# Six float32 units in the first token tile, a shorter pooled attention branch and a split PSUM pool in an attention and two-layer kernel

## The chip, the cores and the metric

The kernel runs on one core of one Trainium2 chip. The metric is the device time of one execution in microseconds (us); the time before is the median of three runs.

## What is computed

```python
q, k, v: (4, 8, 576, 64) float32          # batch, heads, positions, width
# attn(q, k, v): softmax(q @ k.T / 8) @ v
out_d  = attn(q_d, k_d, v_d)              # q_d, k_d, v_d: means of 4 positions (144 rows)
local  = attn(q, k, v) where |i - j| < 4, all other scores -1e9
x = np.repeat(out_d, 4, axis=2) + local   # then laid out as 2304 tokens x 512
h = x @ moe_w_in                          # 512 x 2048, weights arrive as float64
x = softplus(h) @ moe_w_out               # 2048 x 512
h = x @ moe2_w_in
return (h * cos(h)) @ moe2_w_out          # 2304 x 512 float32
```

## The kernel before

**Tiles and stages.** The 2304 tokens lie in five tiles, four of 512 and one of 256. Each of the two layers works a tile in 16 units of 128 hidden columns. One unit is a product into the hidden columns (`unit_in`, "in-unit"), an activation, and a product out of them (`l2` for layer 1, `l4` for layer 2, "out-group": one unit has two halves). A float32 factor is kept as a float16 high part and a float16 low part, and a product of two such factors is made of three float16 products (high by high, high by low, low by high), so that an in-unit is 12 products of 128x128 by 128x512 (L1028) and each half of an out-unit 6 (L1119 in layer 1, L1154 in layer 2).

**Weights.** They arrive as float64 words in `stg` buffers, two units (one block) per DMA. ScalarE rebases a block (L553), VectorE joins the words to float32 (L425, L561), ScalarE sums up a bound (L569), from which a power-of-two scale is fitted (the bounds of four blocks go through a product with an identity, L464, to spread them over the partitions), then ScalarE makes the high half (L440) and VectorE the low one (L436). The first out-group waits for the low halves of W_out's first block.

**Attention.** A pair is two heads of one batch entry; there are 16, `p00` to `p33`, and the first four give tile 0. The stages of one pair, as the code names them: sum1, sum2 (VectorE pools q and k by four, L428, `qt` and `qd`), sum3, sum4 (the same for v), A (local scores, L703 and L707, in windows of 58 rows by 64 keys), A2 to A6 (largest, subtract, exp, sum, normalise), B (pooled scores: three products of 96x144, L761, out of a `qd` whose halves are padded with zeros), B1 to B4, C and D (transposes of the two attention matrices, L809 and L826), E (products with v: pooled L849, windows L860), `up` and E1 (the sum, L874). Tile 0 goes to `raw0`; its scale comes from a bound on v (`vmx`, L693), and is known before the attention is.

**Order.** `Plan` lists operations with estimated costs, works out due times backwards, adds the offsets of the table MOVES, and lists the operations engine by engine; the resulting order of each engine is fixed. Wherever the planner sees TensorE idle it adds a filler, a product of zeros (L1330). POS1 to POS3 say after which unit a later pair is entered in the list. PSUM has three double banks (`any`) and two single ones (`h`). All DMAs are issued by SyncE (SP).

Of the kernel before, what the change touches and what calls it, by code (L numbers as in the profile page):

```python
# [28 lines left out]
RB = 2 * SD // 3  # L29
# [11 lines left out]
POS1 = (6, 10, 15, 20)  # L41
POS2 = (33, 37, 41, 45)
POS3 = (50, 55, 60, 65)
# [14 lines left out]
QKP, VP = (), ()  # L58
YIN = 8
DR4 = 4  # L60
A_W, A_C, A_X, A_G = True, True, True, False
CAP = ("pe", "dve", "act")
OUT0 = 10
IN0 = ((0, 4), (4, 4))

MOVES = {
# [51 lines left out]
class Op:  # L118
    def __init__(self, n, cost, fn, claim, name):
        self.n, self.cost, self.fn, self.claim, self.name = n, cost, fn, claim, name  # L120
        self.succ, self.wait, self.values = set(), 0, set()
        self.key = ""


class Plan:
# [109 lines left out]
    def order(self):  # L235
# [22 lines left out]
        while left:  # L258
            held, started = set(), False
            for op in ready:  # L260
# [18 lines left out]
                if e == "sp":  # L279
                    end = max(dma_free, now + 1.1) + op.cost[e]  # L280
                    dma_free = end
                    free[e] = max(now + 0.45, end - 1.3)
                else:
                    end = now + op.cost[e]
                    free[e] = end
                op.eng, op.start, op.end = e, now, end
# [20 lines left out]
            while done and done[0][0] <= now:  # L307
# [7 lines left out]
                heapq.heappush(done, (end + LAT[op.eng], -1 - n, op))  # L315
                for s in op.succ:
# [41 lines left out]
def build(tc, qk, vw, vd, mask, w1i, w1o, w2i, w2o, out):  # L358
# [3 lines left out]
    with ExitStack() as ctx:  # L362
# [4 lines left out]
        small = ctx.enter_context(tc.tile_pool(name="small", bufs=8))  # L367
# [15 lines left out]
        vmx = const.tile([128, NC_], BF16, name="vmx")  # L383
# [12 lines left out]
        BANK = ring(ps, "any", 3, [128, 2, 512])  # L396
        HB = ring(ps, "h", 2, [128, 512])
# [6 lines left out]
        QT, QD = ring(ap, "qt", 1, [128, 2, SD, 2]), ring(ap, "qd", 2, [128, 3 * SD])  # L404
        VS, SM = ring(ap, "vs", 3, [72, 4, 64]), ring(ap, "sm", NSM, [128, NG, 2, 64])
        ED, AT = ring(ap, "ed", 2, [RB, 3, SD]), ring(ap, "aT", 1, [128, NG, 128])
        AD, UP = ring(ap, "aTd", 1, [72, 2, 2 * SD]), ring(ap, "up", 1, [128, SD])
# [8 lines left out]
        for t in QD.tiles:  # L416
            nc.gpsimd.memset(t[64:128, 0:SD], 0.0)
            nc.gpsimd.memset(t[0:64, SD : 2 * SD], 0.0)
# [35 lines left out]
        def allmax(am, n, red, reads, writes, name):  # L454
# [4 lines left out]

            h = HB.new()  # L460

# [7 lines left out]
            def top():  # L469
                red.append(small.tile([128, 4], F32, tag="red", name="red")[:, 0:n])  # L470
# [29 lines left out]
        class Weight:  # L500
            def __init__(self, name, dram):
                self.name, self.dram, self.first = name, dram, name[1] == "1"
                self.bd, self.s = carr(f"bd_{name}", NB, BF16), carr(f"s_{name}", NF)
# [8 lines left out]

            def hi(self, f, a, n):
                a += 2048 * (f // 2) + 512 * (f % 2)
                return self.t[:, a : a + n]

            def lo(self, f, a, n):
                return self.hi(f, 1024 + a, n)

            def his(self, b):  # L520
                return self.hi(2 * b, 0, 1024).rearrange("p (m e) -> p m e", m=2)

            def los(self, b):
                return self.lo(2 * b, 0, 1024).rearrange("p (m e) -> p m e", m=2)

            def floats(self, b):
                return self.t[:, 2048 * b + 1024 : 2048 * b + 3072].bitcast(F32).rearrange("p (m e) -> p m e", m=2)
# [7 lines left out]
            def decode(self, b, after=()):  # L535
# [30 lines left out]
                def bound():  # L566
# [829 lines left out]
```

## Time and profile before

| | |
|---|---|
| median of 3 runs | 898.52 us (895.9 to 900.05) |
| profiled execution, own time | 899.84 us |
| its span, mean granted TensorE clock | 898.1 us, 0.994 |
| TensorE busy | 870.8 us (97%) |
| weight loads | 453.8 us (51%) |
| VectorE busy | 651.1 us (73%) |
| ScalarE busy | 489.6 us (55%) |
| GpSimd busy | 1.6 us |

The profile is of one execution. Busy time is summed per engine over the whole span, so an engine that sets the pace of one stage can show a low share. TensorE's figure includes the fillers. The clock is the share of full speed that the chip granted to TensorE.

### The profile page before, as it was taken

The numbers are of one execution on the slowest core, as the hardware profiler recorded it, in microseconds if no ns is written. First come the engines' busy times: TensorE is split into PE (matmuls) and PEld (weight loads), VectorE is DVE, ScalarE is ACT, GpSimd is POOL, SyncE is SP. The second block draws the span as 40 slices with busy tenths as digits, with TensorE's granted clock in tenths as the row PEclk, the third lists the DMA queues.
The fourth block names the chain that finished last, engine by engine and source line by source line (L and its number), as shares of the span: only waits on it lengthen the run. The fifth ranks groups of instructions, "written<-read, shape, count | busy, mean of one in ns | idle before, by whom it ended". The sixth has DMA issues, their size and how long they took to land.

```text
span 898.1 us, 14241 instructions
## 1 busy us (share of the span) xinstructions
PE 870.8 (97%) x5699; PEld 453.8 (51%) x5699; DVE 651.1 (73%) x1342; ACT 489.6 (55%) x871; POOL 1.6 (0%) x11
## 2 busy tenths in 40 slices
PE   8888889999999999999999999999999999999997
PEld 4554445445555555444447764444444444445663
DVE  6989999956576856789994764857555675657662
ACT  3579999375453577689966642423234332334331
POOL 0000000000000000000000000000000000000000
PEclk9989999999999999999999999999999999999999
DMA  8764650301222000554400000001000100100001
GB/s 291 242 225 139 239 226 15 94 1 29 58 68 109 1 1 1 188 188 141 141 1 1 2 1 1 0 1 47 1 1 1 47 1 1 48 1 1 1 1 70
DMA packets 13361, 58.87 MB, mean 66 GB/s; under 512 B 1520, under 2 KB 1648, under 8 KB 9200
## 3 DMA queue, kind: packets, MB, share of 16 engines
q1 hardware_dynamic: 13296, 57.97, 18.8%
q8 instruction: 44, 0.72, 0.3%
q14 instruction: 21, 0.17, 0.1%
HBM read 53.25 MB, written 4.72 MB: 65 GB/s over the span
## 4 chain that ended last, share of the span: by engine, by line
PE 77%; ACT 9%; DMA 6%; DVE 6%; issue 1%; SPq 0%; ACTq 0%; DVEq 0%
PE h L1028 35%; PE any L1154 21%; PE any L1119 17%; DMA stg<-w1i 2%; ACT stg L569 2%; DMA stg<-w1o 2%; PE any L860 1%; DMA stg<-w2i 1%; ACT ta L1036 1%; ACT tb L1040 1%; ACT ta L1044 1%; ACT ta L1048 1%; DMA mask_sb<-mask 1%; PE any L761 1%; DVE w1i_t L561 1%
## 5 line engine op out<-in xcount | busy, mean ns | idle before, releaser
L1028 PE MATMUL h<-xt,w1i_t 128*128 128x512 f16 (+1 forms) x960 | 196.7, 358 | 5.5 <-ACT tb L1040 4.5
L1028 PE MATMUL h<-xt,w2i_t 128*128 128x512 f16 (+1 forms) x960 | 198.0, 358 | 0.0
L1154 PE MATMUL any<-w2o_t,g 128*128 128x512 f16 x864 | 197.2, 379 | 0.0
L1119 PE MATMUL any<-g,w1o_t 128*128 128x512 f16 (+1 forms) x864 | 175.4, 355 | 0.0
L1028 PEld LDWEIGHTS <-w1i_t 128*128 128x128 f16 x960 | 93.2, 98 | 97.1 <-issue 6.4
L1028 PEld LDWEIGHTS <-w2i_t 128*128 128x128 f16 x960 | 93.9, 98 | 94.9
L1061 ACT ACTIVATE ta<-h,quarter,i 128x512 f32<-128x512 f32 (+1 forms) x80 | 58.7, 734 | 146.3 <-PE h L1028 142.5
L1119 PEld LDWEIGHTS <-w1o_t 128*128 128x128 f16 x960 | 92.6, 98 | 85.5
L1154 PEld LDWEIGHTS <-g 128*128 128x128 f16 x864 | 84.4, 98 | 98.0
L428 DVE TENSOR_TENSOR g<-td,g 128x512 f16<-128x512 f32 (+1 forms) x152 | 96.2, 633 | 10.8 <-ACT g L446 4.7
L1066 DVE TENSOR_SCALAR tb<-ta 128x512 f32<-128x512 f32 (+1 forms) x80 | 32.0, 400 | 87.6 <-ACT ta L1061 87.4
L1072 ACT ACTIVATE tc<-ta 128x512 f32<-128x512 f32 (+1 forms) x80 | 46.9, 587 | 74.9 <-DVE ta L428 74.6
L1076 DVE SCALAR_TENSOR_TENSOR td<-h,r,tc 128x512 f32<-128x512 f32 (+1 forms) x80 | 55.8, 697 | 32.0 <-ACT tc L1072 29.4
L1036 ACT ACTIVATE ta<-h,i 128x512 f32<-128x512 f32 (+1 forms) x80 | 51.5, 644 | 34.9 <-PE h L1028 31.3
L436 DVE SCALAR_TENSOR_TENSOR td<-ta,sg,tb 128x512 f32<-128x512 f32 (+1 forms) x64 | 43.6, 682 | 23.5 <-ACT ta L1048 22.3
L1048 ACT ACTIVATE ta<-ta,one 128x512 f32<-128x512 f32 (+1 forms) x80 | 54.4, 684 | 1.4
L428 DVE TENSOR_TENSOR ta<-ta,tb 128x512 f32<-128x512 f32 (+1 forms) x80 | 51.1, 638 | 2.4
L1040 ACT ACTIVATE tb<-h,r 128x512 f32<-128x512 f32 (+1 forms) x80 | 51.4, 643 | 0.0
L448 DVE CAST g<-td 128x512 f16<-128x512 f32 (+1 forms) x109 | 42.5, 390 | 8.8 <-PE any L1154 2.6
L1044 ACT ACTIVATE ta<-ta 128x512 f32<-128x512 f32 (+1 forms) x80 | 47.1, 591 | 0.0
L446 ACT ACTIVATE g<-td 128x512 f16<-128x512 f32 (+1 forms) x43 | 26.2, 610 | 17.1 <-DVE td L1076 5.4
L1330 PE MATMUL h<-zero 128*128 128x512 f16 x106 | 30.8, 430 | 3.3 <-POOL zero L1321 2.4
(150 smaller groups left out, 820.7 us busy)
## 6 DMA issues: line engine op xcount, KB each, us to landing
qk<-qk SPq DMA_DIRECT2D x16, 589.0 KB, 5.4
stg<-w1i SPq DMA_DIRECT2D x8, 1024.0 KB, 4.8
stg<-w1o SPq DMA_DIRECT2D x8, 1024.0 KB, 6.6
stg<-w2i SPq DMA_DIRECT2D x8, 1024.0 KB, 6.4
stg<-w2o SPq DMA_DIRECT2D x8, 1024.0 KB, 4.9
vw<-vw SPq DMA_DIRECT2D x16, 320.0 KB, 3.3
vd<-vd SPq DMA_DIRECT2D x16, 288.0 KB
out<-osb SPq DMA_DIRECT2D x18, 256.0 KB, 2.0
```

Source lines behind the costliest of these rows:

```text
L428: eng[e].tensor_tensor(out=out, in0=in0, in1=in1, op=op)
L436: nc.vector.scalar_tensor_tensor(out=out, in0=raw, scalar=s, in1=other, op0=ALU.mult, op1=op)
L1028: nc.tensor.matmul(h.t[:, 0:n], l, r, start=(i == 0), stop=(i == 11))
L1036: act(n, 1, True), lambda: nc.scalar.activation(out=a(), in_=h.t[:, 0:n], func=AF.Abs, scale=col(o.i1, f)),
L1040: act(n, 1, True), lambda: nc.scalar.activation(out=b(), in_=h.t[:, 0:n], func=AF.Relu, scale=col(o.r1, f)),
L1044: act(n), lambda: nc.scalar.activation(out=a(), in_=a(), func=AF.Exp, scale=-1.0),
L1048: act(n, 1), lambda: nc.scalar.activation(out=a(), in_=a(), func=AF.Ln, bias=one),
L1061: act(n, 2, True), lambda: nc.scalar.activation(out=a(), in_=h.t[:, 0:n], func=AF.Identity, scale=col(o.i2, f), bias=quarter), [h, *sc], [ ...
L1072: act(n), lambda: nc.scalar.activation(out=r(), in_=a(), func=AF.Sin, scale=TWOPI),
L1076: dve(n, False, 1), lambda: nc.vector.scalar_tensor_tensor(out=td.t[:, 0:n], in0=h.t[:, 0:n], scalar=col(o.r1, f), in1=r(), op0=ALU.mult, ...
L1119: nc.tensor.matmul(a.t[:, i, 0:n], l, r, start=(first and j == 0), stop=(last and j == 2))
L1154: nc.tensor.matmul(a.t[:, i], l, r, start=(f == 0 and j == 0), stop=(f == NF - 1 and j == 2))
```

## The change

**Float32 units.** With `F0 = 6` the first six units of tile 0 use the joined float32 weights as they are: four float32 products per unit into the hidden columns (`first_in`, L1093), softplus without scales (ScalarE abs, exp, ln; VectorE G into a float32 `g`), and four float32 products per unit out (`first_out`, L1130). Their sum is copied to `xt[0]` ("ypart"), and the scaled sum of the other ten units is added to it. Units 0 and 1 issue their products one at a time (`PARTS = 2`). The weight blocks 0 to 2 of layer 1 are split into halves only after that, for tiles 1 to 4; the places of halves and float32 blocks in the weight tile change accordingly.

**Scale of tile 0.** It is now taken from the largest element of `raw0` (four reductions of 512 columns) in place of the four `vmx` reductions of 640.

**Pooled branch.** sum1 is one operation of 576 columns (was two of 288), sum2 one of 288 (was three of 144); the zeroed halves are gone. B is four products on 64 rows, two of 128x144 (L812) and two of 64x144 (L817). One add and one reciprocal on 13 columns serve both attentions (were four small operations). D's six transposes have 128 columns (were 96).

**Windows.** For batch entries 2 and 3 (`QUADS = 2`) E's window products alternate between the two halves of the rows; A3 becomes two operations and E1 more and smaller ones.

**PSUM.** A fourth double bank is there during the first pairs, in a pool of its own; after the fourth pair's E it is closed and opened again as the two `h` banks. `aT` and `aTd` get a second buffer each.

**Order.** POS1 to POS3 and MOVES are new (one line of many is shown), and the list of out-groups begins with the ten split units of tile 0.

```diff
+F0 = 6
+QUADS = 2
+PARTS = 2
-POS1 = (6, 10, 15, 20)
+POS1 = (1, 2, 4, 8)
...
-    "L1 0 0 ln#1": -56.5, "L1 0 10": -48.5, "L1 0 11": -31, "L1 0 11 exp#1": 132, "L1 0 11 gh#1": -28.5,
...
-                for a in range(2):
-                    two(e, qt.t[:, a], x[:, a, :, 0:2], x[:, a, :, 2:4], ALU.add)
+                two("dve", q, x[:, :, :, 0:2], x[:, :, :, 2:4], ALU.add)
...
-                for t in range(3):
+                for j in range(2):
+                    h = slice(64 * j, 64 * j + 64)
                     nc.tensor.matmul(
-                        bank()[0:RB, SD * t : SD * t + SD], qd.t[:, RB * t : RB * t + RB],
-                        qd.t[:, 2 * SD : 3 * SD], start=True, stop=True,
+                        pb.t[:, j, 0:SD], qd.t[h, 16 * j : 16 * j + 128], qd.t[h, SD : 2 * SD], start=True, stop=True
                     )
...
+                z = slice(64 * side(j, n // 2), 64 * side(j, n // 2) + 64)
...
+        def first_in(f):
...
+            def mm(cs):
+                for c in cs:
+                    nc.tensor.matmul(h.t, W1I.f32(f, 128 * c, 128), raw0[c], start=(c == 0), stop=(c == NC_ - 1))
...
+                    out=u.g(), in0=h.t, scalar=0.0, in1=ta.t, op0=ALU.max, op1=ALU.add
...
+        def first_out(f):
...
+                        nc.tensor.matmul(
+                            a.t[:, i], W1O.f32(f, 128 * (2 * d + i), 128), u.g(), start=first, stop=last
+                        )
...
-            first, last = f == 0, f == NF - 1
+            first, last = f == (0 if t else F0), f == NF - 1
```

The order of TensorE at the first product of tile 0 shows what stands ahead of the layer's first unit. In the names, `qd` and `ed` belong to pooled pairs, `sm` to a local one, `zero` to a filler, `raw` to tile 0; before:

```order
L761 MATMUL any_87<-qd_118 96x144 [waits DVE_49,Activation_49]
L761 MATMUL any_87<-qd_118 96x144 x2
L1330 LDWEIGHTS zero
L1330 MATMUL h_91<-zero 128x512
L1028 LDWEIGHTS w1i_t
L1028 MATMUL h_91<-xt_82,w1i_t 128x512
```

and with the change:

```order
L740 MATMUL any_83<-qk_108 64x64 [waits DMAHW2_49]
L740 MATMUL any_83<-qk_108 64x64 x19
L1093 MATMUL h_775<-raw_150,w1i_t 128x512 [waits DVE_49,PE_49]
L870 MATMUL any_84<-ident,ed_123 72x128 [waits DVE_49]
L870 MATMUL any_84<-ident,ed_123 72x128 x5
L1093 MATMUL h_775<-raw_151,w1i_t 128x512
L853 MATMUL any_85<-ident,sm_121 128x128 [waits Activation_49]
L853 MATMUL any_85<-ident,sm_121 128x128 x4
L1093 MATMUL h_775<-raw_152,w1i_t 128x512
L812 MATMUL any_84<-qd_116 128x144 [waits Activation_49]
L812 MATMUL any_84<-qd_116 128x144
L817 MATMUL any_84<-qd_116 64x144 x2
```

The first unit's products (three of four are shown) now stand one by one between the transposes of one pair and the scores and products of others, and no filler stands behind them; the last filler is six rows ahead of the first.

On VectorE, the operations up to the first low half of W_out (`w1o_t`), before (`td` is an activation, `sm` and `nm` attention, `s_w1o` and `k` scales):

```order
L436 SCALAR_TENSOR_TENSOR td_96<-ta_92,lc_160,tb_94 128x512 [waits DVE_49]
L425 TENSOR_SCALAR ik_167<-k_166 128x1 [waits DVE_49]
L428 TENSOR_TENSOR sm_124<-any_87,nm_219 128x640
L425 TENSOR_SCALAR s_w1o<-lc_160,k_166 128x16
L428 TENSOR_TENSOR xt_85<-td_96,xt_85 128x512 [waits Activation_49]
L724 TENSOR_REDUCE nm_220<-any_88 128x10
L436 SCALAR_TENSOR_TENSOR w1o_t<-w1o_t,s_w1o 128x1024 [waits Activation_49]
L436 SCALAR_TENSOR_TENSOR td_96<-ta_93,lc_160,tb_95 128x512 [waits DVE_49]
```

and with the change (`red` and `sx` belong to the scale of tile 1):

```order
L449 SCALAR_TENSOR_TENSOR td_94<-ta_90,lc_156,tb_92 128x512 [waits DVE_49,Activation_49]
L438 TENSOR_SCALAR s_w1o<-lc_156,k_162 128x10
L461 CAST xt_81<-td_94 128x512 [waits DVE_49]
L764 TENSOR_REDUCE nm_215<-any_83 128x10 [waits PE_49]
L441 TENSOR_TENSOR xt_81<-td_94,xt_81 128x512 [waits DVE_49]
L485 TENSOR_REDUCE red_236<-h_776 128x1 [waits PE_49]
L449 SCALAR_TENSOR_TENSOR w1o_t<-w1o_t,s_w1o 128x1024 [waits Activation_49]
L438 TENSOR_SCALAR sx_176<-red_236 128x1 [waits DVE_49]
```

The low half is the 277th VectorE instruction before, and the 234th with the change.

On TensorE, the place where the first split out-group begins, before:

```order
L703 MATMUL any_89<-mask_sb,ident_b 128x320
L707 MATMUL any_89<-qk_109 64x64 [waits DMAHW2_49]
L707 MATMUL any_89<-qk_109 64x64 x19
L1119 LDWEIGHTS w1o_t [waits Activation_49]
L1119 MATMUL any_87<-g_98,w1o_t 128x512 [waits DVE_49]
```

and with the change:

```order
L1159 LDWEIGHTS w1i_t
L1159 MATMUL h_776<-xt_78,w1i_t 128x512
L1130 MATMUL any_84<-g_100,w1o_t 128x512 x2
L1250 LDWEIGHTS w1o_t [waits Activation_49]
L1250 MATMUL any_85<-g_102,w1o_t 128x512 [waits DVE_49]
```

Where the scores of an attention pair stood ahead of the out-group, an in-unit of tile 0 and float32 out-products stand now; 22 of the 24 float32 out-products stand ahead of it.

## Rows read from the trace of the kernel before

**Rows 1.** The page: span of the profiled execution.
```profile
span 898.1 us, 14241 instructions
```

**Rows 2.** By stretch: sum; busy PE, PEld, DVE, ACT, POOL; TensorE clock, DMA share, GB/s.
```profile
0.00:147.20 147.20, 125.72 (x1326) 72.70 (x1326) 135.92 (x278) 113.37 (x231) 1.64 (x11) 0.97 0.62 210
64.00:147.20 83.20, 73.13 (x725) 40.72 (x722) 81.15 (x154) 80.26 (x158) 0.00 (x0) 1.00 0.49 175
147.90:893.50 745.60, 744.39 (x4343) 380.47 (x4333) 513.60 (x1064) 374.88 (x639) 0.00 (x0) 1.00 0.11 36
```

**Rows 3.** VectorE in order of time near 147 us: start, length, instructions [wait ahead].
```profile
145.96 1.28 DVE L436 SCALAR_TENSOR_TENSOR w1o_t<-w1o_t,s_w1o 128x1024 f16<-128x1024 f32 x1 [0.23 <-ACT w1o_t L440]
147.16 0.75 DVE L436 SCALAR_TENSOR_TENSOR td<-ta,lc,tb 128x512 f32<-128x512 f32 x1
```

**Rows 4.** TensorE in order of time near 148 us; x counts records.
```profile
147.22 0.81 PE L707 MATMUL any<-qk 64*64 64x64 f32 x40
147.96 20.89 PE L1119 MATMUL any<-g,w1o_t 128*128 128x512 f16 x96
168.69 4.05 PE L1119 MATMUL any<-xt,w1o_t 128*128 128x512 f16 x18
```

**Rows 5.** VectorE, groups by form up to 147.2 us: total, mean ns, idle before.
```profile
L436 DVE SCALAR_TENSOR_TENSOR td<-ta,lc,tb 128x512 f32<-128x512 f32 x14 | 10.4, 744 | 0.1
...
L724 DVE TENSOR_REDUCE nm<-any 128x10 f32<-128x640 f32 x10 | 8.2, 820 | 0.0
...
L428 DVE TENSOR_TENSOR qt<-qk 128x288 f32<-128x288 f32 x18 | 7.3, 447 | 4.7 <-DMA qk<-qk 4.7
...
L428 DVE TENSOR_TENSOR qd<-qt 64x144 f32<-64x144 f32 x18 | 5.4, 302 | 0.1
L428 DVE TENSOR_TENSOR g<-td,g 128x512 f16<-128x512 f32 x8 | 5.4, 679 | 0.6 <-ACT g L446 0.5
...
L693 DVE TENSOR_REDUCE vmx<-vw 128x1 bf16<-128x640 f32 x4 | 3.2, 809 | 0.0
...
L739 DVE RECIPROCAL rs<-rs 128x10 f32<-128x10 f32 x8 | 1.7, 212 | 0.0
```

**Rows 6.** TensorE in order of time, first pairs; a float32 product has two records.
```profile
8.43 0.43 PE L703 MATMUL any<-mask_sb,ident_b 128*128 128x320 bf16 x2 [2.00 <-DMA mask_sb<-mask]
...
9.54 2.19 PE L1330 MATMUL h<-zero 128*128 128x512 f16 x5
...
20.96 0.66 PE L826 MATMUL any<-ident,ed 96*72 96x96 f32 x6
21.46 1.46 PE L1330 MATMUL h<-zero 128*128 128x512 f16 x6
22.85 0.72 PE L849 MATMUL any<-aTd,vs 72*64 72x144 f32 x8
23.50 1.49 PE L860 MATMUL any<-aT,vw 64*64 64x58 f32 x44
24.92 1.25 PE L1330 MATMUL h<-zero 128*128 128x512 f16 x5
...
36.02 0.90 PE L761 MATMUL h<-qd 128*96 128x144 f32 x6
36.75 1.24 PE L1330 MATMUL h<-zero 128*128 128x512 f16 x5
```

**Rows 7.** Weight loads, groups by form: total, mean ns, idle before.
```profile
L1028 PEld LDWEIGHTS <-w1i_t 128*128 128x128 f16 x960 | 93.2, 98 | 97.1 <-issue 6.4 <-DVE w1i_t L436 1.3
...
L761 PEld LDWEIGHTS any<-qd 128*96 128x96 f32 x72 | 9.3, 163 | 2.3 <-issue 0.8 <-DVE aT L448 0.2
```

**Rows 8.** What TensorE waited for, 48 to 148 us: total, times, longest.
```profile
PE h L464 <- ACT stg L569: 3.6, 2, 2.6
```

**Rows 9.** By stretch, 48 to 52 us, columns as in rows 2.
```profile
48.00:50.00 2.00, 0.40 (x5) 0.17 (x2) 2.00 (x4) 1.54 (x5) 0.00 (x0) 1.00 0.50 90
50.00:52.00 2.00, 1.00 (x4) 0.39 (x4) 1.96 (x6) 1.77 (x5) 0.00 (x0) 0.66 0.95 381
```

More of the change, by code (lines that the diff above doesn't have):

```diff
@@ L285, in order @@
                     free[e] = end
+                assert all(v.i is not None for v in op.values), op.name
                 op.eng, op.start, op.end = e, now, end
@@ L576, in decode, with bound, total, fit @@
                 P.add(dve(1024), join2, [raw], [x], name=nm + " join2")
-                P.add(act(1024, 1), bound, [x], [("bd", self.name, b), raw], name=nm + " bound")
+                if not self.first:
+                    out = lambda: raw.t.rearrange("p m e -> p (m e)")[:, 0:256].bitcast(BF16)
+                    self.bound(b, out, [raw])
+            def bound(self, b, out=None, held=()):
+                high = b >= self.b0
+                out = out or (lambda: self.part(2 * self.b0 if high else NF).bitcast(BF16))
+                free = ("spare", self.name) if high else ("float", self.name, NB - 1)
+                def total():
+                    with nc.allow_low_precision(reason="a bound, for the choice of a scale"):
+                        nc.scalar.activation(
+                            out=out().rearrange("p (m e) -> p m e", m=2), in_=self.floats(b), func=AF.Abs,
+                            accum_out=self.bd[:, b : b + 1],
+                        )
+                P.add(
+                    act(1024, 1), total, [("float", self.name, b), free], [("bd", self.name, b), *held],
+                    name=f"{self.name}{b} bound",
+                )
             def scale(self, b0, n, then=(), reads=(), writes=()):
+                for a in range(b0, b0 + n, 4):
+                    self.fit(a, min(4, b0 + n - a))
+                steps(then, [("s", self.name, b) for b in range(b0, b0 + n)] + list(reads), writes, "wthen")
+            def fit(self, b0, n):
                 red = []
@@ L590, in scale @@
                 )
-                steps(then, [("s", self.name, b) for b in range(b0, b0 + n)] + list(reads), writes, "wthen")
             def split(self, b):
@@ L701, in A, with pooled, side @@
+            def pooled():
+                nc.scalar.activation(
+                    out=qd.t.rearrange("p (a i) -> p a i", a=2), in_=pa.t[:, :, 64 * NG : 64 * NG + SD], func=AF.Copy
+                )
+            quads = b >= QUADS
+            def side(j, g):
+                return j ^ (g & 1) if quads else j
             def A():
@@ L842, in pair, with runs @@
             u0 = 512 - SD
+            assert not quads or u0 >= 4 * QB
+            def runs(lo, hi):
+                if not quads:
+                    k = int(lo >= cut)
+                    return [(lo, hi, k, lo - cut * k)]
+                out = []
+                for g in range(NG):
+                    x, y = max(lo, 2 * QB * g), min(hi, 2 * QB * g + 2 * QB)
+                    if x < y:
+                        out.append((x, y, g & 1, 2 * QB * (g // 2) + x - 2 * QB * g))
+                return out
             def Em():
@@ new lines, in first_out, with mm @@
+        def first_out(f):
+            u = units[1, 0, f]
+            first, last = f == 0, f == F0 - 1
+            for d in range(2):
+                if first:
+                    accs[d] = BANK.new()
+            for d in range(2):
+                a = accs[d]
+                def mm(a=a, d=d):
+                    for i in range(2):
+                        nc.tensor.matmul(
+                            a.t[:, i], W1O.f32(f, 128 * (2 * d + i), 128), u.g(), start=first, stop=last
+                        )
+                P.add(
+                    pe(1.85), mm, [("float", "w1o", f // 2), *u.keys], [a], [a] if first else [], f"L2 0 {f} {d}"
+                )
+            if last:
+                for d in range(2):
+                    a = accs[d]
+                    y = xt[0][:, 2 * d : 2 * d + 2, :]
+                    P.add(
+                        {**act(1024, 0, True), **dve(1024)}, lambda e, a=a, y=y: copy(e, y, a.t),
+                        [a], [xkey(0, 2 * d), xkey(0, 2 * d + 1)], [], "ypart",
+                    )
@@ L1181, in build, with bounds @@
             pair(b, c)
[L1182 to L1208 removed]
+        def bounds(W, b0, n, *then):
+            for b in range(b0, b0 + n):
+                W.bound(b)
+            W.scale(b0, n, *then)
+        back = [(1, 0, f) for f in range(F0, NF)]
         pos = dict(zip([*POS1, *POS2, *POS3], pairs[4:]))
@@ L1216, in step, with halve, halved @@
             if at in pos:
+                assert pos[at][0] < 2 or (1, 0, NF - 1) not in back
                 pair(*pos[at])
-        for f in range(NF):
-            if f // 2 in dict(IN0) and f % 2 == 0:
-                grp_in(f // 2, dict(IN0)[f // 2])
-            if f == OUT0:
-                grp_out()
+        def halve():
+            HB.free += [0, 1]
+        def halved():
+            px.close()
+            psh = ctx.enter_context(tc.tile_pool(name="psh", bufs=1, space=PSUM))
+            HB.tiles += [psh.tile([128, 512], F32, name=f"h{i}") for i in range(2)]
+        held = BANK.new()
+        P.add({"sp": 0.01}, halved, [], [], [held], "halve", after=outs_of[3:]).hook = halve
+        held.left += 1
+        B0 = F0 // 2
+        for b in range(B0):
+            W1I.decode(b)
+        for b in range(B0, NB):
+            W1I.decode(b)
+        for f in range(F0):
+            first_in(f)
+            step()
+        scale0()
+        for c in range(NC_):
+            split_0(c)
+        then = in_scale(0, F0, NF - F0, W1I, 14) + relu_scale(0, F0, NF - F0, T[0].lc)
+        bounds(W1I, B0, NB - B0, then, [("c", 0)], ["sc0"])
+        for b in range(B0, NB):
+            W1I.split(b)
+        for b in range(B0):
+            W1O.decode(b)
+        for b in range(B0, NB):
+            W1O.decode(b)
+        for f in range(F0, NF):
             unit_in(1, 0, f)
             step()
-        for f in range(NF):
-            l2(0, f)
-            step()
+        bounds(W1O, B0, NB - B0, first_scale(), ["sc0"], [("sc", 0)] + [("s", "w1o", b) for b in range(B0, NB)])
+        for b in range(B0, NB):
+            W1O.split(b)
+        for f in range(F0):
+            first_out(f)
+            step()
+        bounds(W1I, 0, B0)
+        bounds(W1O, 0, B0)
+        for W in (W1I, W1O):
+            for b in range(B0 - 1, -1, -1):
+                W.split(b)
         def x_in(t):
```

416 lines of the change are left out of this document (221 added, 195 removed), and 65 rows, old and new, of the table MOVES.

## Prediction

> **What bounds the kernel now.** I read busy time by stretch first, then what stands on the borders of the stretches. The span is 898.1 us [rows 1], the execution's own time 899.84; the rest outside the span is not touched, so I reckon against 899.84, which is 1.3 above the median of the runs.
>
> From 147.9 us to the end TensorE is busy 744.39 of 745.60 us at clock 1.00 [rows 2]. From there on the time is the sum of TensorE's work, and nothing else can end later. That stretch opens at 147.96 with the first out-group of tile 0 [rows 4]; call this moment T. Before it TensorE is no bound: from 64 to 147.2 us it is busy 73.13 of 83.20 with fillers in it, while VectorE is busy 81.15 and ScalarE 80.26 [rows 2]. What T waits for is VectorE's first low half of W_out, which starts at 145.96 and makes room for the next instruction at 147.16 [rows 3]. So the new time is: new T, plus TensorE's work that is left after it, plus an unchanged tail. Two sums are needed.
>
> Durations become steps by the same place: an instruction of 1.28 us lets the next begin 1.20 later [rows 3], so a VectorE step is the mean less about 0.075.
>
> **Part 1, T by VectorE.** The low half is instruction 277 before and 234 with the change. VectorE was busy 135.92 of 147.2 us up to there [rows 2]; 11.3 us were idle. What changes ahead of it, in steps from the means [rows 5]:
> - pooling q and k cost 2 x (.447 - .075) + 3 x (.302 - .075) = 1.43 per pair, some 9 pairs: 12.9. By those two means 144 columns more cost .145, so one operation of 576 is .447 + .29 = .74, a step of .66; one of 288 is a step of .37. Ten pairs of 1.03: 10.3. This gives -2.6.
> - 16 small operations on normalisers fewer, at about .1 (the reciprocal's .212 is the dearest): -1.7.
> - four maxima over v go (.734 each, -2.9), four over `raw0` come (512 of 640 columns, about .61): -0.5.
> - one A2, one A3, one B1 fewer of what stands ahead (.745 each for the first two, .525 for the third by its 432 of their 640 columns): -2.0.
> - three v-poolings of 512 and two of 256 columns more (.60 by the row of `g`, which has 512 too, and .35): +2.5.
> - float32 units: 13 split G become 7, and six float32 G of the same shape come: 0. Their split into halves falls away: six low parts of .604, one cast (about .35, half of that) and one low half of W_in (1.20) less: -5.2.
> - one maximum of tile 1, one copy of tile 0 and some small operations on scales more: +0.9.
>
> Together -8.6 us. With the same idle time VectorE ends this at 147.2 - 8.6 = 138.6, and T, .8 behind it as before, would be 139.4.
>
> **Part 2, T by TensorE.** This engine now has a chain of its own ahead of T, because the float32 units stand early in its order. The price of a float32 product is not in the trace at 512 columns. Nearest is a float32 product of 144 columns with 128 rows and 96 weight columns: three of them from 36.02 to 36.75, .243 each, 1.69 ns per column [rows 6]. For 512: .865 us. I take this since the passes are of the same kind and run back to back. The low end is a transpose's price: six of 96 columns from 20.96 to 21.46, .87 ns per column, or .44 us [rows 6]. The high end adds the loads in full: a load for 96 columns takes 163 ns [rows 7], by columns .217 for 128, two per product, 1.30 us.
>
> The Trainium skill, page "TensorE: Matmul & The Clock Gate", section "Part 3: Packing small matmuls — row/col tiling", lists as a rule that a weight load overlaps with running matmuls only where its row group differs (though it also names a background buffer for weights). By that rule each load of a full-height product would be paid, 1.30 us each. The trace disagrees for the forms it has: 96 records of float16 products take 20.73 us from 147.96 to 168.69 [rows 4], .216 each, although every one has a load of 98 ns [rows 7], and at L761 six loads of 163 ns do not even fit into the .73 that the three products take.
>
> The first float32 product waits for the attention of tile 0; a transpose right behind it waits for an operation that is instruction 83 on VectorE, whose 83 steps come to 43.3 us, and with the idle time of before ahead of 64 us (11.3 less the 83.20 - 81.15 that fall after it [rows 2], so 9.3) to 52.6 us. From there TensorE does until T:
> - 46 float32 products x .865 = 39.8 (24 in, 22 of 24 out),
> - 10 split in-units x 12 x .216 = 25.9,
> - 3 A x 1.11 (8.43 to 9.54), 4 D x .50 x 128/96, 4 E x 2.07 (.65 from 22.85 and 1.42 from 23.50), 4 C by columns at D's price (.55), 3 B at .5 [rows 6]: 18.0,
> - 15 spreads: .9.
>
> That is 84.6, and ends at 137.2. So both queues come out within about 2 us of each other, VectorE slightly later. Each waits for the other at many places: G for products, products for poolings. Two such chains don't end at the larger one; I add 2.5 us, a quarter of the idle time that VectorE had before. T = 139.4 + 2.5 = 142, a gain of 6.0. ScalarE gets lighter (it loses scale steps of six units and six splits) and I cost it at nothing.
>
> **Part 3, TensorE's work after T.** By the two orders:
> - 72 split out-products fewer (960 to 888) x .216: -15.5. A float32 half unit is dearer (4 x .865 = 3.46) than a split one (12 x .216 = 2.59); the gain is only that this work has moved ahead of T, where TensorE ran fillers.
> - two float32 products are left: +1.7.
> - seven A in place of five: +2.2. Eight D, each .167 dearer: +1.3.
> - B: seven of .73 become eight of .5 (two row halves side by side; .97 if not): -1.1, between -1.1 and +2.6.
> - windows of eight pairs: 1.42 each in the trace [rows 6]. Alternating row halves they could run at the pace of A, where 20 products that alternate take .74 (147.22 to 147.96 [rows 4]); with their greater number .81. I take -4.9; the bounds are 0 and -5.5 (58 columns in place of A's 64).
> - two spreads: +.1.
>
> Sum -16.2. One wait stands against it: tile 1's first unit needs scales that VectorE makes 25.7 us behind the low half, where TensorE has 26.1 us of work. VectorE loses about 1 us in 20 to waits over the whole span ahead of T (11.3 of 147), so I put +1 for it (0 to 3).
>
> **Sum.** -6.0 - 16.2 + 1 = -21.2 us, so the own time is 878.6 and the median of runs about **878**. With the bounds of the terms (float32 .8 to .95, B and windows at their worse end, +2.5 at 0 or 8) this case alone covers 867 to 889.
>
> **The rivals.**
> - *Lock step.* From 64 to 147 us TensorE did only three quarters useful work: its 73.13 us of busy time [rows 2] hold fillers, and without them the products that the order lists come, at the steps above, to some 63.5 of 84 us, because the others fed it too slowly. If the chain of 84.6 us is fed at 85% it takes 99.5 and T is 152, 10 later: 888. At 75% it takes 113, T is 165, and the time 901. For it: every float32 unit goes through ScalarE and VectorE like any other, with only two `h` banks. Against it: up to six units' products don't wait for scales.
> - *Loads are paid.* At 1.30 us per product the chain is 46 x .435 = 20 us longer and ends at 157; with the same 2.5, T is 160, 18 later: 896. Against it stand the loads that were hidden for float16 and at L761 [rows 4, 7]. This is the time that the Trainium skill's rule above gives.
> - *The clock: slower than before.* With no fillers behind the first float32 product, every wait leaves TensorE idle. Before, at 48 to 50 us, TensorE was busy .40 of 2.00 us, waiting 2.6 us for ScalarE's bound [rows 8], and the granted clock went from 1.00 to .66 in the next 2 us [rows 9], in spite of fillers right after. If the whole chain of float32 products runs at the lower level (1.2 GHz), 39.8 us become 79.6: T is 137.2 + 39.8 + 2.5 = 179.5, 37.5 later, and the time 916. It is slower than before once some 23 of the 39.8 us are worked at half the clock (+20.5 on the forecast). Against it: once started, the queue holds 84 us of work with short gaps.
> - *No interlock.* VectorE's steps alone come to 135.9 - 8.6 = 127.3. If pairs that are entered earlier leave it only 2 us idle, and a float32 product steps .7 or less, T is 130: 866.
> - *Windows don't run side by side:* +4.9, inside the first case.
>
> **How the numbers follow.** A measurement of this kernel can tell about 0.5% from no change: faster is below 894, slower above 903. Chances: the forecast .62, all faster. Lock step .18, of which .12 faster, .04 the same, .02 slower. Loads paid .06: .02 faster, .04 same. Clock .08, all slower. No interlock .06, faster. This makes .82, .08 and .10. The range takes the first case with its own bounds, the lower part of lock step and the upper part of the fast case: 865 to 896; outside lie the clock, half of the loads' case and the late part of lock step, under .2.
>
> **What would show it.** In the profile after: first float32 product near 50 us, its step .865 us; VectorE's first low half of W_out near 140, the first split out-group near 142, TensorE busy without gaps at clock 1.00 from there; windows of the last eight pairs about .8 us. It is wrong if that out-group begins after 150, if the clock falls below 1.00 between 55 and 140, if a float32 product steps more than 1.0, or if TensorE has gaps behind the out-group.

## The result, and the profile after

| | before | with the change |
|---|---|---|
| median of 4 runs | 897.52 us | 885.12 us (883.02 to 889.82) |
| ratio, 95% interval | 1 | 0.9867 [0.9818, 0.9915] |
| again, beside the first experiments | 898.16 us | 882.33 us, 0.9825 [0.9804, 0.9847] |

The kernel became faster by 12 us in the first comparison and by 16 us in the second, at intervals of 4 and 2 us to either side. 878 was forecast, inside 865 to 896.

The profiled execution took 886.25 us. Its page:

```profile
span 884.5 us, 14076 instructions
...
PE 868.9 (98%) x5627; PEld 445.2 (50%) x5627; DVE 641.7 (73%) x1290; ACT 484.0 (55%) x870; POOL 0.8 (0%) x7
```

Busy time by stretch, from the first float32 product to the first split out-group and from there to the end (columns as in [rows 2]):

```profile
51.88:146.09 94.21, 89.65 (x636) 45.88 (x631) 88.62 (x161) 83.63 (x147) 0.00 (x0) 0.98 0.55 190
146.09:884.50 738.41, 731.85 (x4374) 370.95 (x4372) 510.51 (x1049) 378.46 (x660) 0.00 (x0) 1.00 0.11 37
```

The kernel before, from its first out-group to the end of its span:

```profile
147.96:898.10 750.14, 744.33 (x4339) 380.46 (x4333) 514.43 (x1064) 375.51 (x640) 0.00 (x0) 1.00 0.11 37
```

This row answers to the second above: behind the out-group TensorE is still the sum, but that sum is shorter. 750.1 us have become 738.4: -11.7. The first row has no counterpart: TensorE, busy 89.65 of 94.21 us, is now nearly full from 52 us on, where it ran fillers before. The out-group itself begins at 146.09 instead of 147.96: -1.9. In the second profile of the same kernel (experiment e0) the two numbers are 737.56 and 143.84, that is -12.6 and -4.1.

VectorE in order of time, its first low half of W_out and the instruction behind it, to be held against [rows 3]:

```profile
140.49 1.28 DVE L449 SCALAR_TENSOR_TENSOR w1o_t<-w1o_t,s_w1o 128x1024 f16<-128x1024 f32 x1
141.68 0.15 DVE L438 TENSOR_SCALAR sx<-red 128x1 int32<-128x1 int32 x1
```

TensorE in order of time, the places that the prediction spoke of:

```profile
51.88 1.12 PE L1093 MATMUL h<-raw,w1i_t 128*128 128x512 f32 x2
...
55.86 0.52 PE L812 MATMUL any<-qd 64*128 64x144 f32 x4
56.30 0.46 PE L817 MATMUL any<-qd 64*64 64x144 f32 x4
56.70 4.56 PE L1093 MATMUL h<-raw,w1i_t 128*128 128x512 f32 x10
...
78.00 3.70 PE L1093 MATMUL h<-raw,w1i_t 128*128 128x512 f32 x8
81.54 0.43 PE L736 MATMUL any<-mask_sb,ident_b 128*128 128x320 bf16 x2
...
94.22 0.72 PE L906 MATMUL any<-aTd,vs 72*64 72x144 f32 x8 [1.61 <-ACT aTd L459]
94.86 1.77 PE L923 MATMUL any<-aT,vw 64*64 64x58 f32 x44
96.57 0.29 PE L479 MATMUL h<-ident_s,bd_w1i 128*128 128x128 bf16 x1
96.65 5.03 PE L1130 MATMUL any<-g,w1o_t 128*128 128x512 f32 x8
101.75 0.82 PE L870 MATMUL any<-ident,ed 128*72 128x128 f32 x6
...
134.66 5.34 PE L1159 MATMUL h<-xt,w1i_t 128*128 128x512 f16 x24 [0.35 <-DVE red L485]
...
144.25 1.88 PE L1130 MATMUL any<-g,w1o_t 128*128 128x512 f32 x4
146.09 1.46 PE L1250 MATMUL any<-g,w1o_t 128*128 128x512 f16 x6
```

Three readings. Four float32 products step from 78.00 to 81.54, .885 us each. The pooled scores (L812 and L817) take from 55.86 to 56.70, .84. And the low half, ready at 141.7, is no longer what the out-group waits for: TensorE's last wait is at 134.66, and it still has queued work until 146.09. The loads of those float32 products (weight loads by form, as in [rows 7]):

```profile
L1093 PEld LDWEIGHTS h<-raw,w1i_t 128*128 128x128 f32 x48 | 8.2, 189 | 8.6 <-issue 6.6 <-DVE g L1114 1.7
```

Two loads of 189 ns per product, .378 together, and yet a step of .885, near the .865 that columns alone give: the loads are hidden, as those of [rows 7] were.

Busy time by stretch around the wait at 94.22, with the granted clock in the third column from the right:

```profile
94.00:96.00 2.00, 1.78 (x46) 1.59 (x47) 2.00 (x3) 2.00 (x4) 0.00 (x0) 1.00 0.14 57
96.00:98.00 2.00, 2.00 (x16) 1.33 (x13) 2.00 (x7) 2.00 (x5) 0.00 (x0) 0.50 0.96 283
98.00:100.00 2.00, 2.00 (x4) 0.77 (x3) 1.39 (x5) 2.00 (x4) 0.00 (x0) 0.65 0.97 370
```

Behind the 1.61 us in which TensorE waited for ScalarE's copy of `aTd`, the granted clock is .50 (the lower of its two levels, 1.2 GHz), then .65 in the mean of the next stretch. The four float32 products from 96.65 take until 101.75, 5.1 us instead of 3.6.

Windows of batch entries 2 and 3, TensorE in order of time:

```profile
200.74 0.91 PE L923 MATMUL any<-aT,vw 64*64 64x58 f32 x44
201.58 1.69 PE L1159 MATMUL h<-xt,w1i_t 128*128 128x512 f16 x7
...
314.07 1.07 PE L923 MATMUL any<-aT,vw 64*64 64x58 f32 x44
315.07 0.77 PE L853 MATMUL any<-ident,sm 128*128 128x128 f32 x5
```

.84 from 200.74 and 1.00 from 314.07, where 1.42 stood in [rows 6].

### The profile page after: what moved, and what is told of

Same layout as the page of the kernel before. It is cut to its first block, busy times and chain, and to the rows that moved or that the text cites. A ratio compares the mean times of both kernels' runs of the same rounds, so it can differ in the third digit from the quotient of the medians.

```text
span 884.5 us, 14076 instructions
## 1 busy us (share of the span) xinstructions
PE 868.9 (98%) x5627; PEld 445.2 (50%) x5627; DVE 641.7 (73%) x1290; ACT 484.0 (55%) x870; POOL 0.8 (0%) x7
## 4 chain that ended last, share of the span: by engine, by line
PE 79%; ACT 7%; DMA 7%; DVE 5%; issue 1%; SPq 0%; ACTq 0%; DVEq 0%
PE h L1159 37%; PE any L1292 21%; PE any L1250 17%; DMA qk<-qk 2%; DMA stg<-w1o 2%; DMA stg<-w1i 2%; DMA stg<-w2i 1%; PE any L923 1%; DMA stg<-w2o 1%; ACT w1i_t L609 1%; ACT w1i_t L453 1%; ACT w1o_t L581 1%; ACT stg L609 1%; PE any L870 1%; PE any L1130 1%
## 5 line engine op out<-in xcount | busy, mean ns | idle before, releaser
L1159 PE MATMUL h<-xt,w1i_t 128*128 128x512 f16 (+1 forms) x888 | 179.6, 356 | 0.3 <-DVE red L485 0.3
L1250 PE MATMUL any<-g,w1o_t 128*128 128x512 f16 (+1 forms) x792 | 160.3, 353 | 0.0
L1159 PEld LDWEIGHTS <-w1i_t 128*128 128x128 f16 x888 | 86.1, 98 | 85.0 <-issue 2.9
L1250 PEld LDWEIGHTS <-w1o_t 128*128 128x128 f16 x888 | 85.2, 98 | 77.8 <-issue 2.0
L441 DVE TENSOR_TENSOR g<-td,g 128x512 f16<-128x512 f32 (+1 forms) x146 | 92.1, 631 | 7.5 <-ACT g L459 0.8
L1167 ACT ACTIVATE ta<-h,i 128x512 f32<-128x512 f32 (+1 forms) x74 | 46.9, 634 | 23.4 <-PE h L1159 19.1
L1179 ACT ACTIVATE ta<-ta,one 128x512 f32<-128x512 f32 (+1 forms) x74 | 49.7, 675 | 1.4
L1171 ACT ACTIVATE tb<-h,r 128x512 f32<-128x512 f32 (+1 forms) x74 | 46.9, 634 | 4.7 <-DVE td L449 3.6
L1175 ACT ACTIVATE ta<-ta 128x512 f32<-128x512 f32 (+1 forms) x74 | 42.9, 581 | 0.1
L453 ACT ACTIVATE xs<-xt,sx 128x512 f16<-128x512 f32 (+1 forms) x23 | 15.2, 661 | 21.0 <-DVE xt L1066 14.2
```

The costliest lines, as they stand in the source:

```text
L441: eng[e].tensor_tensor(out=out, in0=in0, in1=in1, op=op)
L1159: nc.tensor.matmul(h.t[:, 0:n], l, r, start=(i == 0), stop=(i == 11))
L1167: act(n, 1, True), lambda: nc.scalar.activation(out=a(), in_=h.t[:, 0:n], func=AF.Abs, scale=col(o.i1, f)),
L1171: act(n, 1, True), lambda: nc.scalar.activation(out=b(), in_=h.t[:, 0:n], func=AF.Relu, scale=col(o.r1, f)),
L1175: act(n), lambda: nc.scalar.activation(out=a(), in_=a(), func=AF.Exp, scale=-1.0),
L1179: act(n, 1), lambda: nc.scalar.activation(out=a(), in_=a(), func=AF.Ln, bias=one),
```

## The experiments

All runs were compared with the kernel before on the same chip; a ratio of .001 is .9 us.

| run | median us | ratio to before, 95% |
|---|---|---|
| e0, the change again | 882.33 | 0.9825 [0.9804, 0.9847] |
| e1, windows on one side | 887.89 | 0.9878 [0.9857, 0.9900] |
| e4, seven fillers | 884.66 | 0.9852 [0.9831, 0.9872] |
| e5, entry 1 alternating, new order | 889.29 | 0.9897 [0.9880, 0.9914] |
| e2, 12 products more | 890.76 | 0.9918 [0.9900, 0.9935] |
| e3, 12 G more | 888.53 | 0.9893 [0.9873, 0.9913] |
| e9, 12 abs more | 888.17 | 0.9892 [0.9872, 0.9912] |
| e10, entry 1 alternating, order kept | 883.27 | 0.9827 [0.9801, 0.9852] |
| e6, before without offsets | 903.06 | 1.0070 [1.0049, 1.0091] |
| e7, the change without offsets | 896.64 | 0.9999 [0.9983, 1.0015] |
| e8, no float32 unit, no offsets | 932.65 | 1.0398 [1.0374, 1.0421] |
| e12, eight float32 units, no offsets | 899.37 | 1.0022 [1.0002, 1.0041] |

The theory behind them: the gain lies in TensorE's sum behind the out-group, and ahead of the out-group the engines hold each other up, so that work saved on any one of them is paid back only in part.

**e0, the mark.**

> The changed kernel unchanged, as the mark for the runs beside it: 883 to 888 us by both theories, first split out-group near 146 us.

The median is .7 us below the expected range, and the out-group came at 143.84, 2 us earlier than expected. The two stretches are as in the first profile. Below, "the front" is the one from the first float32 product to the first split out-group (here 93.65 us), "the rest" is the one from there to the end (737.56):

```profile
50.19:143.84 93.65, 89.55 (x635) 46.39 (x630) 88.27 (x161) 83.64 (x147) 0.00 (x0) 0.98 0.55 189
143.84:881.40 737.56, 731.85 (x4374) 370.86 (x4372) 510.56 (x1049) 378.73 (x660) 0.00 (x0) 1.00 0.11 37
```

**e1, windows on one side.**

```diff
-                return j ^ (g & 1) if quads else j
+                return j
...
```

> The windows of batch entries 2 and 3 go back to one row half per head and to their former order; every other instruction keeps its place. Theory (TensorE is the sum behind the first split out-group, so what its instructions take is paid in full): windows step .84 (entry 2) and 1.0 (entry 3) in the changed kernel and 1.42 before, so 4 x .58 + 4 x .42 = +4.0 us, all of it behind 146 us. Rival (the alternation has no part in the gain, or another engine hides it): windows as now, below +1 us.

Measured: +.0053 against e0, +4.8 us. The two stretches of its profile:

```profile
51.23:141.83 90.60, 87.52 (x635) 45.20 (x631) 88.14 (x161) 83.60 (x147) 0.00 (x0) 1.00 0.56 196
141.83:883.50 741.67, 736.22 (x4374) 375.38 (x4372) 510.92 (x1049) 378.51 (x660) 0.00 (x0) 1.00 0.11 37
```

The rest grew from 737.6 to 741.7, +4.1, the theory's +4.0. The first row has a second use: as many instructions as in e0, but no wait over 1.5 us and clock 1.00 throughout, and the stretch takes 90.60 us with TensorE busy 87.52, against 89.65 at clock .98 in the first profile. So what the fall of the clock cost there is about 2 us. It also shows how far the front scatters with its order kept: 90.6 us here, 93.7 in e0, 94.2 in the first profile.

**e4, fillers ahead of the wait.**

```diff
+FILL, FILLED = {"p12 E#1": 7}, []
...
+                if e == "pe" and FILL.get(op.key[1]):
+                    for _ in range(FILL[op.key[1]]):
+                        x = self.filler()
...
+                            out.append(x)
```

> Seven zero products stand ahead of the one E that waited 1.6 us at 94 us for ScalarE, after which the granted clock was 0.50 from 96 to 98 and 0.65 from 98 to 100 us. Theory (TensorE now ends last ahead of the first split out-group, and the gap cost it the clock): clock 1.00 there, four float32 products from 96.6 us take 3.6 instead of 5.1 us, out-group 1.5 to 2 us earlier, time -1 to -2 us. Rival (VectorE ends last there, TensorE has slack): clock 1.00, but the out-group where it is, within 0.5 us. Second rival (the clock fell for another reason): clock as now, and the fillers' time of up to 0.3 us lost.

Measured: 884.66, beside 882.33 of e0; their intervals overlap. TensorE in order of time:

```profile
82.84 0.22 PE L487 MATMUL h<-ident_s,am 128*128 128x128 bf16 x1 [2.04 <-DVE g L1122]
82.89 3.63 PE L1138 MATMUL any<-g,w1o_t 128*128 128x512 f32 x4
...
92.71 1.67 PE L1492 MATMUL h<-zero 128*128 128x512 f16 x7
94.31 0.72 PE L914 MATMUL any<-aTd,vs 72*64 72x144 f32 x8
```

and the clock by stretch:

```profile
84.00:86.00 2.00, 2.00 (x3) 0.78 (x3) 2.00 (x6) 1.49 (x5) 0.00 (x0) 0.50 0.92 387
94.00:96.00 2.00, 2.00 (x45) 1.49 (x44) 0.71 (x2) 2.00 (x5) 0.00 (x0) 1.00 0.90 377
96.00:98.00 2.00, 2.00 (x21) 1.22 (x19) 1.30 (x7) 1.66 (x4) 0.00 (x0) 1.00 0.31 73
```

At the place that was mended the clock stayed at 1.00, and from E's start to the first split in-unit it took 7.1 us instead of 8.2. But in this execution a wait of 2.04 us stood at 82.84, for a G of VectorE, and the clock fell behind that one. The front took 94.26 us all the same. In the first profile and in e0, the two without fillers that waited at this place (1.61 and 1.98 us), the clock fell to .50 behind the wait. That products of zeros kept it up is likely, but rests on this one execution, since not every wait of this length was followed by a lower clock (the last section has two that were not). That fillers at this one place bring time is not shown.

**e5, alternating windows for entry 1 too.**

```diff
-QUADS = 2
+QUADS = 1
```

> Alternating row halves for batch entry 1 too (four pairs between 61 and 115 us); A3 in two operations and E1 in more pieces for them, and the planner orders anew. Theory (TensorE ends last from 52 us on): four windows .5 to .6 us shorter, -2 us, less what the smaller VectorE operations take, so -2 to 0. Rival (VectorE ends last there): its some 12 more small operations at .1 to .2 us each make it 1 to 2 us later: +1 to +2.

Measured +.0072 against e0, +6.5 us, outside what either theory gave. The stretch behind the out-group:

```profile
147.57:892.70 745.13, 738.24 (x4395) 373.69 (x4393) 514.89 (x1056) 385.62 (x671) 0.00 (x0) 1.00 0.11 36
```

The rest is 745.1, 7.6 us more than with e0, and TensorE is busy 6.4 us more in it: the planner put other work there, a split in-unit and some float32 out-products among it. This profile is of the slowest of seven executions, 894.52 where the median is 889.29, so its sizes are not those of the median. The loss looks like one of order, which e10 tests.

**e2, e3, e9: which engine's time is paid ahead of the out-group.** Each repeats one instruction of the float32 units, with the order kept.

```diff
+                for _ in range(2 * (cs[0] == 0)):
+                    nc.tensor.matmul(h.t, W1I.f32(f, 0, 128), raw0[0], start=True, stop=True)
```

> Two float32 products more in each of the six float32 in-units, nothing moved: 12 x .885 = 10.6 us more work for TensorE ahead of the first split out-group. Theory 1 (TensorE alone ends last there): first float32 product to first split out-group 94 + 10.6 = 105 us, time +10 to +11. Theory 2 (VectorE ends last, TensorE fills its gaps of 4 to 5 us first): +4 to +6. Theory 3 (the engines go in lock step, each waits for the others in turn): close to the full price, +8 to +11, the gaps not used up.

```diff
+            def G():
+                for _ in range(3):
+                    nc.vector.scalar_tensor_tensor(
+                        out=u.g(), in0=h.t, scalar=0.0, in1=ta.t, op0=ALU.max, op1=ALU.add
+                    )
...
```

> G of the six float32 units is done three times in place of once, nothing moved: 12 x .67 = 8.0 us more for VectorE ahead of the out-group. Theory 1 (TensorE alone): below +3, by the latency of single waits. Theory 2 (VectorE alone): +8. Theory 3 (lock step): +5 to +8.

```diff
+            def ab():
+                for _ in range(3):
+                    nc.scalar.activation(out=ta.t, in_=h.t, func=AF.Abs)
...
```

> The first ScalarE step of the six float32 units is done three times, nothing moved: 12 x about .53 = 6.4 us more for ScalarE. ScalarE was busy 83.6 of the 94.2 us ahead of the out-group. Theories 1 and 2: it has some 10 us of slack, below +2. Theory 3 (lock step of all three engines): +3 to +6.

Against e0: +8.4, +6.1 and +6.0 us, each with some 2.5 us to either side, for 10.6, 8.0 and 6.4 us of added work by the expectations. Against the first comparison (.9867) it is 3.8 us less each; but e0 and e10, the latter from the same set of runs as these three, agree on .9825 and .9827, and the interval of the first comparison is twice as wide. The front of e2, of e3 and of e9 by stretch, one row each:

```profile
52.15:151.49 99.34, 97.64 (x659) 49.75 (x654) 88.66 (x161) 84.25 (x147) 0.00 (x0) 1.00 0.52 179
```

```profile
49.99:148.00 98.01, 91.50 (x635) 46.14 (x630) 96.07 (x173) 83.29 (x147) 0.00 (x0) 0.97 0.52 180
```

```profile
52.17:148.60 96.43, 89.25 (x637) 45.70 (x631) 88.29 (x161) 90.59 (x159) 0.00 (x0) 0.98 0.52 184
```

The front is 99.3, 98.0 and 96.4 us, where e0 has 93.65: +5.7, +4.4, +2.8 in one profile each. Since the front without added work took 90.6 to 94.3 us (e1, e4), one profile cannot size this; e1 and e2, the two at clock 1.00 throughout, are 8.7 us apart. VectorE is busy 7.8 us more in e3 than in e0, ScalarE 7.0 more in e9. So by the medians against e0 every engine's added time is paid for the greater part, ScalarE's too. Theory 1 and theory 2, which leave ScalarE some 10 us of slack, gave less than +2 for e9, and theory 1 less than +3 for e3; the three results lie in the ranges of theory 3. What these runs don't tell apart: the repeated instructions stand in the chain of steps of each float32 unit (products, abs, exp, ln, G, products), so what is paid can be the length of this chain as well as the time of a full engine. The traces speak for the chain in part: from e0 to e9 ScalarE's waits for the weights' DMAs fall from 9.2 to 3.6 us, which is room for most of the added 7.0, and still TensorE's waits for G of VectorE grow from .9 to 4.4 us. The same work outside the chain was not tried.

**e10, entry 1 alternating with the order kept.** In the code A3 issues two instructions and E1 six for entry 1, inside the same operations of the planner.

```diff
-            quads = b >= QUADS
+            quads, quads_ = b >= 1, b >= QUADS
...
```

> Alternating row halves for batch entry 1 with the planner's order kept: per pair A3 is issued as two instructions and E1 as six, nothing else moves. TensorE -4 x .5 to .6 = -2.2 us, VectorE +4 x 5 x .075 = +1.5 us, all ahead of the first split out-group. Theory 1 (TensorE alone): -2. Theory 2 (VectorE alone): +1.5. Theory 3 (lock step): between, -1 to +1. And if the +7 us of the run with the planner's own new order came from the row halves themselves and not from that order, +7 here too.

Measured: .9827 against e0's .9825, no difference.

```profile
52.01:144.99 92.98, 86.82 (x636) 43.40 (x630) 89.24 (x180) 83.41 (x147) 0.00 (x0) 0.98 0.55 191
```

TensorE is busy 86.82 instead of 89.55, VectorE 89.24 instead of 88.27, and the stretch hardly shorter: what TensorE saved came back as waits for VectorE, the longest 2.4 us for a G. The +6.5 of e5 was the order, not the row halves. Neither run is better than the change itself.

**e6, e7, e8, e12: without the table of offsets.**

```diff
-MOVES = {
...
+MOVES = {}
```

> The kernel before with an empty table of offsets. Theory (the gain is one of structure: TensorE's work ahead of the first split out-group in place of fillers): the offsets are worth a few us in either kernel, 900 to 915 here. Rival (the gain is that of newly fitted offsets): the kernel before without offsets is about as fast as the changed one without them.

> The changed kernel with an empty table of offsets. Theory: 10 to 16 us below the kernel before without offsets, the rest behind the first split out-group 12 us shorter as with offsets, plus new gaps. Rival: within 4 us of it.

> The changed kernel with no float32 unit (F0 = 0; all 16 units of tile 0 split) and no offsets. Theory: 72 split out-products come back behind the first split out-group and 2 float32 ones go, +13.8 us; ahead of it TensorE has 40 us of float32 less and 15.5 of split in-products more, but VectorE and ScalarE have the splits of six units back: 8 to 16 us slower than the changed kernel without offsets. Rival (the shorter pooled branch and the alternating windows make the gain, the float32 units none): within 3 us of it.

> Eight float32 units in place of six, no offsets. Two more units: behind the first split out-group 24 split out-products fewer, -5.2 us; ahead of it +2 x (3.54 - 2.59) for the in-units and +2 x 3.54 for the out-units, +9.0 us of TensorE work, and some 3 us less for VectorE and ScalarE. Theory (TensorE has hardly a gap left ahead of it with six): 0 to +4 against six without offsets. Rival (there are gaps left to fill): -2 to -5.

Without offsets the change is .0071 faster than the kernel before without offsets, 6.4 us: between the two theories. Their profiles tell the halves apart. Up to the out-group and behind it, e6:

```profile
0.00:147.31 147.31, 124.17 (x1358) 70.94 (x1359) 137.12 (x281) 110.74 (x219) 1.64 (x11) 0.98 0.63 210
147.31:900.80 753.49, 746.23 (x4345) 381.59 (x4343) 522.14 (x1072) 369.13 (x643) 0.00 (x0) 1.00 0.11 37
```

The front and the rest of e7:

```profile
52.27:157.77 105.50, 98.42 (x688) 49.17 (x686) 88.72 (x156) 84.56 (x150) 0.00 (x0) 0.95 0.50 171
157.77:899.00 741.23, 734.34 (x4394) 372.60 (x4391) 519.33 (x1069) 369.21 (x640) 0.00 (x0) 1.00 0.11 37
```

Behind the out-group 753.5 became 741.2, -12.3, the same gain as with offsets (750.1 to 737.6 or 738.4). Ahead of it, the out-group moved from 147.3 to 157.8, +10.5, with clock .95 and TensorE fillers and waits among the 105.5 us. This profile of e7 is of its slowest execution, 900.81, 4.2 us above the median; the medians, 6.4 us apart, leave about +6 ahead of the out-group if the rest is the same. So the structure brings the 12 us behind the out-group in both orders tried, and the fitted order is what keeps the float32 work ahead of it from costing some 6 to 10.

e8, with `F0 = 0` and the old scaled copy of tile 0's result, in the stretch of its largest loss and behind its out-group, which begins at 180.91:

```profile
168.00:185.00 17.00, 11.57 (x44) 4.59 (x43) 16.88 (x31) 12.97 (x17) 0.00 (x0) 0.80 0.00 0
180.91:933.40 752.49, 739.39 (x4264) 371.57 (x4263) 490.46 (x1009) 352.35 (x608) 0.00 (x0) 0.99 0.10 35
```

It lost 36 us against e7, far more than the 8 to 16 expected. In the two profiles 11.3 of them are the rest (752.5 against 741.2). That is near the 13.8 that the products give, but by chance in part: the 72 products are back (672 full-width ones behind the out-group, 600 in e7), yet TensorE is busy only 5.1 us more there (739.39 against 734.34), because other work, three A among it, now stands ahead of the late out-group; the other 6.2 are waits. The 23 ahead of it are an out-group that starts at 180.9, behind 28 fillers in a row and waits of 2.6 and 2.7 us for tile 1's `xt`: a poor order of its own, made by a planner whose list was arranged for float32 units. How much a fitted order would win back was not tried, so e8 rules out that the units are worth nothing in this order, and does not size them.

e12, eight float32 units:

```profile
52.90:158.81 105.91, 101.35 (x655) 50.69 (x654) 87.11 (x148) 85.38 (x152) 0.00 (x0) 1.00 0.47 164
158.81:896.30 737.49, 730.08 (x4409) 370.89 (x4406) 518.86 (x1071) 364.86 (x633) 0.00 (x0) 1.00 0.11 38
```

The rest fell by another 3.7 us (5.2 expected), and the out-group came 1.0 later than in the profile of e7. The medians give +.0023, 2 us slower than with six, with intervals that overlap: eight units are not faster. With 3.7 us saved behind the out-group this means some 6 us more ahead of it; the two profiles show less, since the one of e7 is 4.2 us above its median and this one 1.3 below. The gaps ahead of the out-group are used up, as the theory had it.

What the shorter pooled branch, the second buffers of `aT` and `aTd` and the split PSUM pool bring by themselves was not run.

## Why the prediction was right, and where its terms were off

The forecast gain of 21.2 us came to 13.6 in the spans of the two profiles (898.1 to 884.5). The 7.6 that are missing are 4.1 at the start of the out-group and 3.7 in TensorE's sum behind it, less .2 of the 1 us that was added for a wait; both errors go the same way, so the hit is not owed to errors that cancel.

**The bound behind the out-group** was right: 731.85 of 738.41 us busy. The 72 fewer products are there, full-width out-products behind the first split out-group, before and with the change:

```profile
L1119 PE MATMUL any<-g,w1o_t 128*128 128x512 f16 x672 | 153.0, 379 | 0.0
```

```profile
L1250 PE MATMUL any<-g,w1o_t 128*128 128x512 f16 x600 | 138.2, 379 | 0.0
```

And so is the mechanism: work moved into a time in which TensorE ran fillers.

**TensorE's sum behind it** was forecast at -16.2 and came to -12.5 (busy 744.33 to 731.85). By terms: the products (-15.5 and +1.7), A (+2.2) and D (+1.3, .66 a step against .50) held. B failed: the step "two row halves side by side" at .5 is .84 in the trace, so eight of them against seven of .73 give +1.6 instead of -1.1; it lies inside the bounds that were given. The windows brought 4.0 instead of 4.9, confirmed by e1. With these the terms sum up to -12.6. Of the +1 for tile 1's scales TensorE paid at most .8: its idle time in this stretch is 5.8 us before and 6.6 (5.7 in e0) after.

**The out-group's start** was forecast at 142 and came at 146.1 and 143.8. The forecast took it that the out-group waits for VectorE's low half, .8 us behind its end. That was misread in the trace before: the low half was done at 147.24, and TensorE, without a gap from its in-units on, came to the out-group .7 us later by its own queue, which [rows 4] continues from 147.22:

```profile
139.08 7.93 PE L1028 MATMUL h<-xt,w1i_t 128*128 128x512 f16 x36
146.85 0.43 PE L703 MATMUL any<-mask_sb,ident_b 128*128 128x320 bf16 x2
```

The part by VectorE was near: the low half ends at 141.7 (139.4 in e0), 138.6 was forecast. The step that failed is "VectorE slightly later", with a TensorE chain of 84.6 us. The chain starts as forecast (51.88, 52.6 forecast) but takes 94.2 and 93.7 us: .9 for 46 products at .885 instead of .865, 1.0 for three B, about 2 for the clock behind one wait, 4.6 and 4.1 us of waits, and the rest in small items. In the profiles with this front (the first, e0, e1, e4) the out-group starts 5.6 us behind the start of the low half and 4.4 behind its end, where .8 was taken: TensorE, not VectorE, ends last there.

**ScalarE at nothing** was wrong: in e9 time added to it is paid as VectorE's is in e3. It was busy 83.6 of the 94.2 us and waited another 10.1 for the weights' DMAs, and of TensorE's 4.6 us of waits 2.8 are put down to it in the trace (1.6 of them for `aTd`): the other engines wait for single steps of it, whatever its sum.

**The price of a float32 product** was right: .885 measured, .865 forecast from 144 columns. The rule of the Trainium skill (page "TensorE: Matmul & The Clock Gate", section "Part 3: Packing small matmuls — row/col tiling") that was weighed there would have made it 1.30; here the loads of full-height float32 products are hidden, and this case's measurement decides.

**The rivals.** Lock step was named, and it is the right description of the front (e2, e3, e9, e10): 84.6 us of work took 94.2, 9.6 more, between the 4.8 that the forecast left to TensorE's chain (52.6 to 142) and the 15 of this rival. It came out in full, with the out-group at 158, only where the order was not fitted (e7). One of the prediction's own signs of being wrong came: the clock fell below 1.00 between 55 and 140, to .50 and .65 from 96 to 100 us. What that rival feared did not follow: it cost about 2 us and not 37, since the clock was back at 1.00 from 100 us on. Loads paid and idle row halves of the windows did not come.

## What to carry to other kernels

Work that moves from a full engine's stretch into one with fillers brings its own length there, once; read the size of the gaps in the other stretch first, since they limit how much can be moved (six units fill them, eight are no better). Where three engines are each about 90% busy in a stretch, the largest of their sums is too low a forecast: here 84.6 us of TensorE's work took 94.2, and time added to a step of the float32 units on any of the three cost .7 to .9 of itself beside e0 (.3 to .4 beside the wider first comparison). And a structural gain and the order that was fitted to it are two things: without the offsets of either kernel the change gave about half, 6.4 us.

## What was not expected of the hardware

- Products that use different row halves do not always run side by side. A's 64x64 products with alternating halves and windows in four quarters do: 22 windows (44 records) take .84 us, .038 each, where 58 columns at the 1.69 ns of a float32 product alone would be .098. B's two of 64 rows by 128 columns take .44 together, hardly less than two of .243 one after the other, and its two of 64x64 take .40. Why is open; it was not tried.
- A wait of 1.6 to 2 us can be enough for the granted clock to be .50 to .65 in the next stretches of 2 us, although TensorE had been busy right before it (1.61 us in the first profile, 1.98 in e0, 2.04 in e4). It need not be: a wait of 1.67 us in e10, up to 100.78, left the clock at 1.00, and so did one of 1.92 in e9:

```profile
69.75 1.12 PE L1093 MATMUL h<-raw,w1i_t 128*128 128x512 f32 x2 [1.92 <-DVE g L1115]
```

```profile
70.00:72.00 2.00, 2.00 (x11) 0.84 (x11) 2.00 (x4) 1.94 (x5) 0.00 (x0) 1.00 0.39 106
```

  What tells the two cases apart was not tried.
